# One decode layer: the second pair's keys in two loads, and two never-taken branches placed earlier

## The chip, the core and the metric

The kernel runs on one core of a Trainium2 chip. A core has a matrix engine (TensorE, PE), a vector engine (VectorE, DVE), a scalar engine (ScalarE, ACT), a general engine (GpSimd, POOL) and SyncE (SP), which issues most loads here. Each engine works through its own list of instructions, and semaphores order them. 16 DMA engines move data between the main memory and the on-chip buffer. The metric is the device time of one execution in microseconds (us); lower is better.

## The reference

One token goes through an attention block with a key and value cache, then through a block B with a second normalisation and an MLP:

```python
x = A_x                                               # 1 x 512
h = x + _A_ref(_layernorm(x), A_k_cache, A_v_cache, A_wq, A_wo)
h2 = h + _B_ref(_layernorm(h), B_w1, B_w2, B_w3, B_w4)
# _A_ref: q = x @ wq (32 heads of 128); 8 key/value heads, each serves 4 query heads
scores = einsum("bhqd,bhkd->bhqk", q, k) * (Dh ** -0.5)   # 16384 positions
p = softmax(scores); o = einsum("bhqk,bhkd->bhqd", p, v); return o @ wo
# _B_ref
hs = concatenate([g0, g1, g2, g3]) @ w2               # shifts by one and two places along the sequence
x1 = x + hs
h2 = gelu(_layernorm(x1) @ w3) @ w4                   # 512 -> 1792 -> 512
return x1 + h2
```

The sequence has one place, so every shift in block B brings in zeros alone: `hs` is zero, and `w1` and `w2` are not needed. What has to be read is the key cache and the value cache, 8 heads of 16384 x 128 values in bfloat16 each, and `wq`, `wo`, `w3` and `w4`.

## The kernel before

**Order of the work.** The functions `dve`, `act`, `pool`, `pe` and `load` append operations to one list per engine (class `Program`). When all are appended, `emit` finds which operation waits for which, and `_run` writes each engine's list out, with semaphore waits ahead of an operation where it needs them. `_vector` writes VectorE's list. `_tensor` writes TensorE's, where the four pairs of heads are a real loop over the block `pe_pair`, with inner loops over two halves and eight pieces; what stands after the loop is straight code. Nothing reorders the lists: an engine that waits holds up what is behind it in its list.

**Branches that are never taken.** At the start of their lists VectorE and TensorE mark a place for a branch hint. At the end of its list each of the two has a compare-and-branch whose condition never holds (a register that is zero, or positive, is compared with "less than 0") and which names an earlier block as its target (`body`, `pe_pair`). The hint marked at the start belongs to this branch (L146 and L315).

**Stages.** After `wq` has landed, TensorE forms the queries (L596). Then there are four pairs of key/value heads (`PAIRS`), j = 0 to 3. A pair's keys and its values are 8 MB each, 64 KB in each of 128 partitions. For one pair:

- Keys. Buffer `kb` holds a whole pair, as two halves `kb[0]` and `kb[1]`. For each half, VectorE transposes the keys into the single buffer `kt` (L619, four instructions of two pieces each; eight of one piece in the last half of the last pair), and TensorE multiplies them with the queries, piece by piece (L633, after a clearing product, L627).
- Softmax (L644 to L659): maximum on VectorE, a product on TensorE, exponential on ScalarE, transposes on VectorE.
- Values. TensorE multiplies the weights with the values in buffer `vb` (L669), in four parts.
- Gathering (L685 to L693), and a copy of the next pair's queries, `qn` (L701).

**Tail.** Products with `wo` (L735), the sums and the statistics (L739 to L539), products with `w3` (L753), the activation (L765), transposes (L769), products with `w4` (L774: 14 blocks m of four products), the last sum (L778) and the store of the output (L780).

**Loads.** SyncE issues them in the order of its list, each when its buffer is free: `wq`, the keys of pair 0 in two halves, values 0, keys 1, values 1, keys 2, values 2, keys 3, values 3 in four parts, `wo` in two, `w3`, and `w4` in three (blocks 0 to 9, 10 to 12, and 13). `wq` shares `vb` with the values. `wo` goes into `kb[0]`, `w3` and `w4` into `kb[1]`. A half of `kb` is free when VectorE has transposed all of it. `load_keys(j + 1, y)` stands behind the work of half y of pair j. For the pairs listed in `WHOLE`, it does nothing for y = 0, and for y = 1 it loads both halves with one transfer that all later transposes wait for:

```python
WHOLE = (1,)
...
if j in WHOLE:
    if y:
        load("k0", kb_all[:, :], pair_rows(A_k_cache, j), ("r", 0, 0),
             also=[("r", h, i) for h in range(2) for i in range(RPARTS)])
    return
load(f"k{y}", kb[y][:, :], pair_rows(A_k_cache, j)[:, y * n:(y + 1) * n], ("r", y, 0), ...)
```

The helper `more`, with which TensorE could repeat a product in a small loop, is defined and not called.

Of the kernel before, what the change touches and what calls it, by code (L numbers as in the profile page):

```python
# [12 lines left out]


class Op:
    __slots__ = ("eng", "fn", "deps", "sem", "val", "needed", "dma", "at", "worth", "times", "own")

    def __init__(self, eng, fn, deps, dma, at, worth, times, own):
        self.eng, self.fn, self.deps, self.dma, self.at = eng, fn, deps, dma, at
        self.worth, self.times, self.own = worth, times, own  # L20
        self.sem = self.val = None
        self.needed = False


class Program:
# [17 lines left out]
    def part(self, *mark):  # L43
        self.mark, self.count = mark or None, {}

    def op(self, eng, fn, r=(), w=(), bank=(), dma=None, worth=1, times=1, own=None):
        deps = []

        def need(o, raw):
            if o is None:  # L50
                return
            if o.eng == eng and o.dma is None and (eng == "PE" or not raw):
                return
            deps.append(o)

        for k in r:
            need(self.last_w.get(k), True)
        for k in w:
            need(self.last_w.get(k), False)
            for o in self.readers.get(k, {}).values():  # L60
                need(o, False)
        for k in bank:
            for e, o in self.users.get(k, {}).items():
                if e != eng:
                    need(o, False)
        at = None
        if self.mark is not None:
            n = self.count[eng] = self.count.get(eng, -1) + 1
            at = (*self.mark, n)
        o = Op(eng, fn, deps, dma, at, worth, times, own)  # L70
        for k in r:
            self.readers.setdefault(k, {})[(eng, dma)] = o
        for k in w:
            self.last_w[k] = o
            self.readers[k] = {}
        for k in bank:
            self.users.setdefault(k, {})[eng] = o
        if dma is not None:
            if dma not in self.dma_sems:
                self.dma_sems[dma] = self.ctx.enter_context(self.nc.semaphore(f"d_{dma}"))  # L80
                self.dma_count[dma] = 0
            self.dma_count[dma] += 16
# [57 lines left out]
    def _vector(self):  # L140
        eng = self.nc.vector
        rv = eng.alloc_register("never")
        hint = eng.mark_branch_hint_location()
        eng.reg_mov(rv, 0)
        self._run(eng, self.ops["DVE"], {})
        eng.br_lt(rv, 0, "body", "pe_query").branch_hint(hint)  # L146

    def _tensor(self):
        nc, eng, ops = self.nc, self.nc.tensor, self.ops["PE"]
        inside = [n for n, o in enumerate(ops) if o.at is not None]  # L150
        lo, hi = inside[0], inside[-1] + 1
        at = {o.at: o for o in ops[lo:hi]}
# [53 lines left out]
        sem, v0, _ = told[0, 0]  # L206
# [4 lines left out]
        r, rl, ry, rq, rk = (eng.alloc_register(n) for n in ("seen", "landed", "half", "query", "piece"))  # L211
        hint = eng.mark_branch_hint_location()
        eng.reg_mov(r, first - step * last)
        eng.reg_mov(rl, v0 - 1)
        seen = {}
# [81 lines left out]
        nc.switch_bb("pe_after", parent=None)  # L297
        seen[id(vector)] = final
        seen[id(sem)] = told[last, parts - 1][2]
        n = 0  # L300
        for o in ops[hi:]:
            if o.times == 1:
                self._run(eng, [o], seen)
                continue
            eng.reg_mov(ry, 0)
            eng.br(f"pe_more{n}")
            nc.switch_bb(f"pe_more{n}", parent=None)
            assert not o.needed
            self._run(eng, [o], seen)
            eng.reg_add(ry, ry, 1)  # L310
            eng.br_lt(ry, o.times, f"pe_more{n}", f"pe_less{n}")
            nc.switch_bb(f"pe_less{n}", parent=None)
            n += 1

        eng.br_lt(rl, 0, "pe_pair", "pe_end").branch_hint(hint)  # L315
        nc.switch_bb("pe_end", parent=None)

D = 512
HQ = 32
# [9 lines left out]
W3 = ((0, 4),)  # L329
W4 = ((0, 10), (10, 13), (13, 14))  # L330
PAIRS = HKV // 2
WHOLE = (1,)
RPARTS = 6
QPAD = 4 * 7
QW = QPAD + 128
# [4 lines left out]
def bass_sequential_preLN__gqa_block_cached__mixer_s_mlp__decode_kernel(  # L340
# [13 lines left out]
    with ExitStack() as ctx:  # L354
        sb = lambda name, shape, dt: ctx.enter_context(nc.sbuf_tensor(name, shape, dt))
        ps = lambda name, shape, dt: ctx.enter_context(nc.psum_tensor(name, shape, dt))
        P = Program(nc, ctx)
# [30 lines left out]
        qb = sb("qb", [128, 4, PAIRS, QW], BF16)  # L388
# [35 lines left out]
        O_ps = [banks[:, 2, :], banks[:, 3, :]]  # L424
# [4 lines left out]
        def load(name, dst, src, key, by="SP", also=()):  # L429
            P.op(by, lambda e: e.dma_start(dst, src), w=[key, *also], dma=name)  # L430

        def pair_rows(src, j):
            return src[0, 2 * j:2 * j + 2].rearrange("g (u t) d -> (g u) (t d)", u=64)

        def load_keys(j, y):
            n = 128 * DH
            if j in WHOLE:
                if y:
                    load("k0", kb_all[:, :], pair_rows(A_k_cache, j), ("r", 0, 0),
                         also=[("r", h, i) for h in range(2) for i in range(RPARTS)])  # L440
                return
            load(f"k{y}", kb[y][:, :], pair_rows(A_k_cache, j)[:, y * n:(y + 1) * n], ("r", y, 0),
                 also=[("r", y, i) for i in range(1, RPARTS)])

# [24 lines left out]
        def pe(fn, r=(), w=(), bank=()):  # L469
            return P.op("PE", fn, r, w, bank)  # L470

        def piece(cuts, m):
            return [lo <= m < hi for lo, hi in cuts].index(True)

        def more(n):

            P.op("PE", lambda e: e.matmul(O_ps[1][:, :], qb[:, 0, 0, 0:128], kt[:, 0:512], start=True, stop=True),
                 r=["qb", ("kt", 0)], w=[("O", 1)], bank=[("O", 1)], times=n)

        def copies(col, n):  # L480

# [45 lines left out]
        def inverse_root(i, n, by):  # L527
# [7 lines left out]
            for k in range(3):  # L535
# [31 lines left out]
            r=["hT", (("st", 0), 0), (("st", 0), 6)], w=["xn"])  # L567
# [25 lines left out]
        for i, key in enumerate(keys):  # L593
            P.part("query", i)
            for k in range(NCH):
                pe(lambda e, k=k: e.matmul(banks[:, bass.ds(P.b, 1), :], copies(xn[:, k:k + 1], 128),  # L596
                                           wq_k[:, k, bass.ds(P.c, REP * DH)], start=(k == 0), stop=(k == NCH - 1)),
                   r=["xn"] + [("v", x) for x in range(4)], w=["n" if key == "mn" else key], bank=[key])
        P.part()
        for g in range(2):  # L600
            row = banks[64 * g:64 * g + 64, PAIRS * g:PAIRS * g + PAIRS, :].rearrange("p j c -> p (j c)")
            for b in range(2):
# [122 lines left out]
        for n, (lo, hi) in enumerate(W4):  # L725
# [4 lines left out]
            r=["o_m"], w=["o_f"])  # L730
        dve(lambda e: e.tensor_copy(o_b[:, :], o_f[:, :]), r=["o_f"], w=["o_b"])

        for r_ in range(32):
# [3 lines left out]
               r=["o_b", ("r", 0, piece(WO, r_))], w=[("O", 0)], bank=[("O", 0)])  # L737
        h_ps, hkey = s_ps[:, 1, :], ("s", 1)
        dve(lambda e: e.tensor_copy(osum[:, :], O_ps[0][:, :]), r=[("O", 0)], w=["osum"], bank=[("O", 0)])  # L739
        for q in range(4):  # L740
            pe(lambda e, q=q: e.matmul(h_ps[32 * q:32 * q + 32, 0:128], copies(row32[:, 0:1], 32),
                                       osum[:, q * 128:(q + 1) * 128], start=True, stop=True),
               r=["osum", "row32"], w=[hkey], bank=[hkey])
# [4 lines left out]
            r=["hT", (S, 0)], w=["hc"])  # L748


        for k in range(NCH):
            for q in range(4):
                pe(lambda e, k=k, q=q: e.matmul(s_ps[32 * q:32 * q + 32, 0, 0:FQ], hc[:, k, :],  # L753
                                                w3_sb[:, k, q * FQ:(q + 1) * FQ], start=(k == 0), stop=(k == NCH - 1)),
                   r=["hc", ("r", 1, piece(W3, k))], w=[("s", 0)], bank=[("s", 0)])
# [5 lines left out]
            r=["hr", (S, 0), (S, 6)], w=["xs"])  # L761
        pool(lambda e: e.tensor_tensor(xsum[:, :], hr[:, :], xs[:, :], ALU.add), r=["hr", "xs"], w=["xsum"])
        for n in range(2):
            lo, hi = n * NHC // 2, (n + 1) * NHC // 2
            act(lambda e, lo=lo, hi=hi: e.activation(  # L765
                hg[:, :].rearrange("p (i m) -> p i m", m=NHC)[:, :, lo:hi],
                s_ps[:, 0, 0:FQ].rearrange("p (i m) -> p i m", m=NHC)[:, :, lo:hi],
                ACTF.Gelu_apprx_tanh, scale=s[:, 7:8]), r=[("s", 0), (S, 7)], w=[("hg", n)], bank=[("s", 0)])
            dve(lambda e, lo=lo, hi=hi: e.transpose(  # L769
                hcol[:, lo:hi, :].rearrange("p m u -> p (m u)"),  # L770
                hg[:, :].rearrange("p (i m) -> p m i", m=NHC)[:, lo:hi, :]), r=[("hg", n)], w=[("hcol", n)])
        for m in range(NHC):
            for o in range(4):
                pe(lambda e, m=m, o=o: e.matmul(  # L774
                    n_ps[32 * o:32 * o + 32, 0:128], hcol[:, m, :], w4_sb[:, m, o * 128:(o + 1) * 128],
                    start=(m == 0), stop=(m == NHC - 1)),
                   r=[("hcol", 2 * m // NHC), ("r", 1, 2 + piece(W4, m))], w=["n"], bank=["mn"])
        dve(lambda e: e.tensor_tensor(fin[:, :], xsum[:, :], n_ps[:, 0:128], ALU.add),  # L778
            r=["n", "xsum"], w=["fin"], bank=["mn"])
        P.op("SP", lambda e: e.dma_start(out[0, 0:1, :].rearrange("o (q j) -> (o q) j", q=4), fin[0:128:32, :]),  # L780
             r=["fin"], w=["out"], dma="out")
# [32 lines left out]
```

## Time and profile before

| | |
|---|---|
| median of 3 runs | 200.2 us (200.03 to 200.45) |
| profiled execution | 199.21 us, of which the span from the first to the last instruction is 196.6 us |
| mean granted TensorE clock | 0.85 of full speed |
| busy in the span | PE 114.1 us, DVE 118.0 us, ACT 9.0 us, POOL 7.3 us |
| DMA | 79.18 MB, mean 403 GB/s over the span |

A profile row of work has the start or a group's count, the engine, the line of the kernel (L619 is line 619), the operation and its operands: `kt<-kb` writes `kt` from `kb`. `[7.63 <-DMA kb...]` is the idle time of the engine ahead of the row and what ended it. The chain that ended last goes back from the last instruction, at each step to what released it. Rows of 40 digits cut the span into 40 equal slices, with the busy share in tenths. All times in the rows count from the start of the span.

### The profile page before, as it was taken

To read this page: it belongs to the slowest core of one execution; us is meant where nothing else is said; L and a number is where in the kernel's file an instruction comes from. 1 tells how busy PE (TensorE), PEld (TensorE's weight loads), DVE (VectorE), ACT (ScalarE), POOL (GpSimd) and SP (SyncE) were. 2 spreads that over 40 slices of the span, in tenths; PEclk is the share of its full clock that TensorE was granted. 3 is DMA by queue.
4 is the path that set the end of the run, shared out by engine and by line. 5 is a ranking of instruction groups with operands and counts; after the bars stand their busy time and mean duration, and the time that the engine had idled before them with its cause. 6 is when DMAs were issued, how large, how long until landed. Compare 5 with 4: busy or idle time off the path is not lost.

```text
span 196.6 us, 2321 instructions
## 1 busy us (share of the span) xinstructions
PE 114.1 (58%) x693; PEld 44.4 (23%) x693; DVE 118.0 (60%) x155; ACT 9.0 (5%) x15; POOL 7.3 (4%) x16
## 2 busy tenths in 40 slices
PE   0129619888165009988255598860928888346533
PEld 0113203233021003423022132320403323112212
DVE  6740799990534049991453999635079992452371
ACT  3000000000200000000200000002000000130020
POOL 7100000000000000000000000000000000000041
PEclk9999987999859755999859799996696999958975
DMA  6999999999999999998999999999999999999800
GB/s 227 467 453 427 447 427 527 427 427 440 427 427 427 427 427 427 427 427 367 460 433 433 440 427 427 427 420 433 427 427 417 427 427 430 442 400 423 342 0 2
DMA packets 3041, 79.18 MB, mean 403 GB/s; under 512 B 352, under 2 KB 480, under 8 KB 608
## 3 DMA queue, kind: packets, MB, share of 16 engines
q1 hardware_dynamic: 3032, 79.17, 94.0%
q14 instruction: 1, 0.01, 0.0%
q10 hardware_dynamic: 8, 0.00, 0.0%
HBM read 79.17 MB, written 0.00 MB: 403 GB/s over the span
## 4 chain that ended last, share of the span: by engine, by line
DVE 35%; PE 33%; DMA 20%; issue 8%; ACT 2%; ACTq 0%; DVEq 0%; SPq 0%
DVE kt L619 21%; PE banks L633 17%; DMA kb<-in_A_k_cache_dram 14%; PE banks L669 8%; DMA vb<-in_A_wq_dram 6%; PE banks L596 5%; DVE pt L659 4%; DVE mx L644 2%; ACT p_sb L655 2%; DVE od L688 2%; PE banks L735 1%; PE banks L774 1%; PE banks L647 1%; DVE qcol L603 1%; PE banks L691 1%
## 5 line engine op out<-in xcount | busy, mean ns | idle before, releaser
L633 PE MATMUL banks<-kt,qn 128*128 x256 | 70.5, 411 | 23.1 <-DVE kt L619 16.9
L619 DVE STREAM_TRANSPOSE kt<-kb 128x2048 int32<-128x2048 int32 (+1 forms) x36 | 70.9, 2037 | 7.6 <-DMA kb<-in_A_k_cache_dram 7.6
L633 PEld LDWEIGHTS banks<-kt,qn 128*128 x256 | 26.1, 102 | 66.1 <-issue 52.8
L669 PE MATMUL banks<-vb,pt 128*32 128x512 bf16 x256 | 20.7, 495 | 0.0
L644 DVE TENSOR_REDUCE mx<-banks 128x1 f32<-128x1024 f32 x4 | 4.9, 1224 | 20.2 <-PE banks L633 20.2
L659 DVE STREAM_TRANSPOSE pt<-p_sb 64x1024 bf16<-64x1024 bf16 x8 | 9.9, 1239 | 5.4 <-ACT p_sb L655 5.3
L685 DVE TENSOR_SCALAR od<-banks,rowc 128x128 f32<-128x128 f32 x4 | 1.4, 350 | 19.5 <-PE banks L669 19.5
L596 PE MATMUL banks<-vb,xn 128*128 x32 | 9.2, 461 | 6.1 <-DMA vb<-in_A_wq_dram 6.1
L655 ACT ACTIVATE p_sb<-banks,bias 128x1024 bf16<-128x1024 f32 x4 | 4.5, 1114 | 164.6 <-DVE nmh L651 164.6
L676 PE MATMUL banks<-acc,zd 128*32 128x1 f32 x8 | 1.1, 202 | 17.7 <-DVE pt L659 17.7
L669 PEld LDWEIGHTS banks<-vb,pt 128*32 128x32 bf16 x256 | 8.1, 121 | 10.7 <-issue 7.6
L603 DVE STREAM_TRANSPOSE qcol<-banks 64x1024 f32<-64x1024 f32 x4 | 4.8, 1228 | 8.6 <-PE banks L596 8.6
L627 PE MATMUL banks<-qn 128*128 128x512 bf16 x8 | 3.1, 387 | 7.3 <-DVE qn L701 6.3
L534 POOL TENSOR_SCALAR st<-st 128x1 f32<-128x1 f32 x1 | 0.2, 242 | 182.9 <-DVE st L519 182.9
L596 PEld LDWEIGHTS banks<-vb,xn 128*128 128x128 bf16 x32 | 3.7, 115 | 11.2 <-issue 9.0
L647 PE MATMUL banks<-mxd,mean 128*128 128x128 f32 x8 | 2.0, 326 | 6.6 <-DVE mxd L645 6.6
L691 PE MATMUL banks<-od,zo 128*32 128x128 f32 x8 | 1.6, 285 | 6.5 <-DVE od L688 6.5
L676 PEld LDWEIGHTS banks<-acc,zd 128*32 128x32 f32 x8 | 0.7, 140 | 18.4 <-DVE pt L659 18.4
L688 DVE SCALAR_TENSOR_TENSOR od<-banks,rowc,od 128x128 f32<-128x128 f32 x12 | 4.2, 351 | 0.4
L556 DVE CAST ident<-ident_f 4x4 bf16<-4x4 f32 x1 | 3.8, 3848 | 0.6 <-POOL ident_f L551 0.6
L559 PE MATMUL banks<-x,quarter 4*128 4x128 bf16 x1 | 0.3, 285 | 6.0 <-DVE quarter L557 6.0
L627 PEld LDWEIGHTS banks<-qn 128*128 128x128 bf16 x8 | 0.8, 95 | 10.5 <-issue 10.5
(76 smaller groups left out, 44.0 us busy)
## 6 DMA issues: line engine op xcount, KB each, us to landing
kb<-in_A_k_cache_dram SPq DMA_DIRECT2D x6, 4096.0 KB, 21.7
vb<-in_A_v_cache_dram SPq DMA_DIRECT2D x4, 2048.0 KB, 19.4
vb<-in_A_wq_dram SPq DMA_DIRECT2D x1, 4096.0 KB, 12.4
kb<-in_A_wo_dram SPq DMA_DIRECT2D x1, 3072.0 KB, 21.2
kb<-in_B_w_dram SPq DMA_DIRECT2D x1, 1792.0 KB, 19.0
kb<-in_B_w_dram SPq DMA_DIRECT2D x1, 1280.0 KB, 21.7
kb<-in_A_wo_dram SPq DMA_DIRECT2D x1, 1024.0 KB, 23.3
kb<-in_B_w_dram SPq DMA_DIRECT2D x1, 384.0 KB, 22.2
```

What stands on the lines that cost most here:

```text
L556: dve(lambda e: e.tensor_copy(ident[:, :], ident_f[0:4, 0:4]), r=["ident_f"], w=["ident"])
L596: pe(lambda e, k=k: e.matmul(banks[:, bass.ds(P.b, 1), :], copies(xn[:, k:k + 1], 128), wq_k[:, k, bass.ds(P.c, REP * DH)], start=(k == 0) ...
L603: dve(lambda e, g=g, b=b, row=row: e.transpose(qcol[64 * g:64 * g + 64, 2 * b:2 * b + 2, :, :].rearrange("p e m u -> p (e m u)"), row.rear ...
L619: P.op("DVE", lambda e, view=view: e.transpose(view(kt), view(kb[y])), r=[("r", y, i) for i in range(RPARTS)], w=[("kt", t + i) for i in r ...
L627: pe(lambda e: e.matmul(s_ps[:, bass.ds(P.y, 1), :], copies(none, 128), copies(none, 512), start=True, stop=False, skip_group_check=True), ...
L633: pe(lambda e, n=n: e.matmul(s_ps[:, bass.ds(P.y, 1), :], qn[:, n, bass.ds(P.q, 128)], ktv[:, n // 2, n % 2, :, bass.ds(P.k, 8), :], start ...
L644: dve(lambda e: e.tensor_reduce(mx[:, :], s_all, AX.X, ALU.max), r=[("s", 0), ("s", 1)], w=["mx"], **both)
L647: pe(lambda e: e.matmul(m_ps[:, 0:128], mean4[:, :], mxd[:, :], start=True, stop=True), r=["mxd", "mean4"], w=["m"], bank=["mn"])
L655: act(lambda e: e.activation(p_sb[:, :], s_all, ACTF.Exp, bias=bias[:, 0:1], scale=float(SCALE), accum_out=acc[:, :]), r=[("s", 0), ("s", ...
L659: dve(lambda e, g=g: e.transpose(pt[64 * g:64 * g + 64, :, :, g, :], p_sb[64 * g:64 * g + 64, :]), r=["p"], w=["pt"])
L669: pe(lambda e, x=x, l=l, ct=ct, ch=ch: e.matmul(O_ps[0][32 * ct:32 * ct + 32, :], pt[:, 8 * x + l, ch, :, :].rearrange("p g u -> p (g u)") ...
L688: dve(lambda e, block=block, c=c: e.scalar_tensor_tensor(od[:, :], block, rowc[:, c:c + 1], od[:, :], ALU.mult, ALU.add), r=[key, "rowc", ...
```

## The change

The keys of pair 1 are loaded as those of the other pairs: one transfer per half, each with its own semaphore, the first behind the work of half 0 of pair 0, the second behind that of half 1. The never-taken branches, with the hints that belong to them, no longer stand at the end: VectorE's stands behind its transposes of the activation and ahead of the last sum, TensorE's ahead of block 10 of the products with `w4`. Operations without a function, `dve(None)` and `pe(None)`, mark the two places in the lists. The unused helper `more`, the field `times` and the code that wrote its loop are gone.

```diff
     def _vector(self):
...
-        self._run(eng, self.ops["DVE"], {})
-        eng.br_lt(rv, 0, "body", "pe_query").branch_hint(hint)
+        ops, seen = self.ops["DVE"], {}
+        on = next(n for n, o in enumerate(ops) if o.fn is None)
+        self._run(eng, ops[:on], seen)
+
+        eng.br_lt(rv, 0, "body", "ve_on").branch_hint(hint)
+        self.nc.switch_bb("ve_on", parent=None)
+        self._run(eng, ops[on + 1:], seen)
...
-        n = 0
-        for o in ops[hi:]:
-            if o.times == 1:
-                self._run(eng, [o], seen)
-                continue
...
-        eng.br_lt(rl, 0, "pe_pair", "pe_end").branch_hint(hint)
-        nc.switch_bb("pe_end", parent=None)
+        on = next(n for n, o in enumerate(ops) if o.fn is None)
+        self._run(eng, ops[hi:on], seen)
+
+        eng.br_lt(rl, 0, "pe_pair", "pe_on").branch_hint(hint)
+        nc.switch_bb("pe_on", parent=None)
+        self._run(eng, ops[on + 1:], seen)
...
-WHOLE = (1,)
...
         def load_keys(j, y):
             n = 128 * DH
-            if j in WHOLE:
-                if y:
-                    load("k0", kb_all[:, :], pair_rows(A_k_cache, j), ("r", 0, 0),
-                         also=[("r", h, i) for h in range(2) for i in range(RPARTS)])
-                return
...
+        dve(None)
         for m in range(NHC):
+            if m == W4[1][0]:
+                pe(None)
             for o in range(4):
```

More of the change, by code (lines that the diff above doesn't have):

```diff
@@ L15, with __init__ @@
 class Op:
-    __slots__ = ("eng", "fn", "deps", "sem", "val", "needed", "dma", "at", "worth", "times", "own")
-    def __init__(self, eng, fn, deps, dma, at, worth, times, own):
+    __slots__ = ("eng", "fn", "deps", "sem", "val", "needed", "dma", "at", "worth", "own")
+    def __init__(self, eng, fn, deps, dma, at, worth, own):
         self.eng, self.fn, self.deps, self.dma, self.at = eng, fn, deps, dma, at
-        self.worth, self.times, self.own = worth, times, own
+        self.worth, self.own = worth, own
         self.sem = self.val = None
@@ L44, in part, with op @@
         self.mark, self.count = mark or None, {}
-    def op(self, eng, fn, r=(), w=(), bank=(), dma=None, worth=1, times=1, own=None):
+    def op(self, eng, fn, r=(), w=(), bank=(), dma=None, worth=1, own=None):
         deps = []
@@ L69, in op @@
             at = (*self.mark, n)
-        o = Op(eng, fn, deps, dma, at, worth, times, own)
+        o = Op(eng, fn, deps, dma, at, worth, own)
         for k in r:
@@ L299, in _tensor @@
         seen[id(sem)] = told[last, parts - 1][2]
-        n = 0
-        for o in ops[hi:]:
-            if o.times == 1:
-                self._run(eng, [o], seen)
-                continue
[L305 to L313, printed above, removed]
-        eng.br_lt(rl, 0, "pe_pair", "pe_end").branch_hint(hint)
-        nc.switch_bb("pe_end", parent=None)
+        on = next(n for n, o in enumerate(ops) if o.fn is None)
[3 more added lines that the diff above has]
+        self._run(eng, ops[on + 1:], seen)
 D = 512
@@ L473, in piece @@
             return [lo <= m < hi for lo, hi in cuts].index(True)
-        def more(n):
-            P.op("PE", lambda e: e.matmul(O_ps[1][:, :], qb[:, 0, 0, 0:128], kt[:, 0:512], start=True, stop=True),
-                 r=["qb", ("kt", 0)], w=[("O", 1)], bank=[("O", 1)], times=n)
         def copies(col, n):
```

## The prediction

> **What bounds the kernel now.** I read the page first: its span, the granted clock, the DMA row and the shares of the chain that ended last.
>
> ```profile
> span 196.6 us, 2321 instructions
> PEclk9999987999859755999859799996696999958975
> DMA  6999999999999999998999999999999999999800
> DVE 35%; PE 33%; DMA 20%; issue 8%; ACT 2%; ACTq 0%; DVEq 0%; SPq 0%
> ```
>
> Two things run through the whole span. The DMA engines are busy from the second slice to the 38th of 40, so the stream of loads never pauses. And the chain is mostly DVE and PE, with 20% DMA. The chain in order of time tells where that DMA is: besides the opening load there is one piece, and its landing ends the only long DVE idle time with a DMA as its releaser. Next the rows of VectorE from the timeline (start, length, instruction; in brackets the idle time before it).
>
> ```profile
> 44.23 27.01 DMA kb<-in_A_k_cache_dram
> ```
> ```profile
> 26.51 17.66 DVE L619 STREAM_TRANSPOSE kt<-kb 128x2048 int32<-128x2048 int32 x8
> 63.41 0.30 DVE L701 COPY qn<-qb 128x624 bf16<-128x624 bf16 x1
> 71.34 17.66 DVE L619 STREAM_TRANSPOSE kt<-kb 128x2048 int32<-128x2048 int32 x8 [7.63 <-DMA kb<-in_A_k_cache_dram]
> 108.14 0.32 DVE L701 COPY qn<-qb 128x624 bf16<-128x624 bf16 x1
> 108.37 17.65 DVE L619 STREAM_TRANSPOSE kt<-kb 128x2048 int32<-128x2048 int32 x8
> 145.38 0.32 DVE L701 COPY qn<-qb 128x624 bf16<-128x624 bf16 x1
> 145.62 17.89 DVE L619 STREAM_TRANSPOSE kt<-kb 128x2048 int32<-128x2048 int32 x12
> 193.58 0.29 DVE L778 TENSOR_TENSOR fin<-xsum,banks 128x128 bf16<-128x128 f32 x1 [1.32 <-PE banks L774]
> ```
>
> Pair 1's key transposes wait for one 8 MB load, which lands at 44.23 + 27.01 = 71.24. From there on no pair waits for keys: the transposes of pairs 1, 2 and 3 start at 71.34, 108.37 and 145.62, some 37.1 us apart, which is the pace of DVE and PE. So whatever moves 71.34 moves the end, until the stream of loads stops it. Where it stops it is read from the issues (SP's rows of the timeline) and, below them, from the DMA view in one small window around each issue (the last number is the time from issue to landing).
>
> ```profile
> 23.00 0.33 SPq L430 DMA_DIRECT2D vb<-in_A_v_cache_dram  x1
> 61.18 0.33 SPq L430 DMA_DIRECT2D vb<-in_A_v_cache_dram  x1
> 80.31 9.05 SPq L430 DMA_DIRECT2D kb<-in_A_k_cache_dram  x2
> 105.80 0.33 SPq L430 DMA_DIRECT2D vb<-in_A_v_cache_dram  x1
> 117.33 9.10 SPq L430 DMA_DIRECT2D kb<-in_A_k_cache_dram  x2
> 154.57 0.81 SPq L430 DMA_DIRECT2D kb<-in_A_wo_dram  x2
> 163.59 1.75 SPq L430 DMA_DIRECT2D kb<-in_B_w_dram  x4
> ```
> ```profile
> vb<-in_A_v_cache_dram SPq DMA_DIRECT2D x1, 28.9
> vb<-in_A_v_cache_dram SPq DMA_DIRECT2D x1, 29.4
> kb<-in_A_k_cache_dram SPq DMA_DIRECT2D x1, 4096.0 KB, 20.0
> kb<-in_A_k_cache_dram SPq DMA_DIRECT2D x1, 4096.0 KB, 21.0
> vb<-in_A_v_cache_dram SPq DMA_DIRECT2D x1, 23.7
> kb<-in_A_k_cache_dram SPq DMA_DIRECT2D x1, 4096.0 KB, 21.8
> kb<-in_A_k_cache_dram SPq DMA_DIRECT2D x1, 4096.0 KB, 22.8
> kb<-in_A_wo_dram SPq DMA_DIRECT2D x1, 1024.0 KB, 23.3
> kb<-in_B_w_dram SPq DMA_DIRECT2D x1, 1792.0 KB, 19.0
> kb<-in_B_w_dram SPq DMA_DIRECT2D x1, 1280.0 KB, 21.7
> kb<-in_B_w_dram SPq DMA_DIRECT2D x1, 128.0 KB, 22.1
> ```
>
> Issue plus time gives the landings. A row of two issues that is 9.05 long has its second one 0.33 before its end, so at 89.03; likewise 126.10, 154.94 (0.44 long) and 164.91 (0.43 long, the last of four, whose second is at 163.96). Values 0 land at 51.9, values 1 at 90.6, keys 2 at 100.3 and 110.0, values 2 at 129.5, keys 3 at 139.1 and 148.9, the last part of wo at 178.2, w3 at 182.6, the first w4 part at 185.7 and the last at 187.0. They land in the order of issue, and at the size's own pace: a half of the keys every 9.7 us, the whole of pair 1 in 71.2 - 51.9 = 19.3. That is a line of transfers served one after the other, always with a next one waiting. An earlier issue cannot make this line shorter; it can only let work start on what has landed.
>
> **The keys in halves.** Removed: one issue of 8 MB at 44.23, after the last transposes of pair 0. Added: an issue of the first half when the first four transposes of pair 0 are done, 26.51 + 17.66/2 = 35.3 (the same step in pair 1: 71.34 + 8.83 = 80.2, issue at 80.31), and the second half at 44.23 as before. On SP that is one more issue, 0.33 us; the next thing behind it waits until 44.23 anyway, so it costs nothing. DVE's second half gets one more semaphore wait, on a landing that is earlier than its turn (below).
>
> Both halves stand in the line behind values 0, so they land at 51.9 + 9.7 = 61.6 and 71.2, where the whole landed before. DVE is free for them after qn at 63.41; transposes start 0.24 after qn does (108.14 to 108.37, 145.38 to 145.62), so at 63.65 instead of 71.34: a gain of 7.69. The first half lasts until 72.5, when the second has been there for 1.3 us. Between them the halves could also break the line; the bound from rows is 9.7 us a half against 19.3 the whole, at most 0.1 us, and I take nothing.
>
> The Trainium skill, DMA: Bandwidth & Descriptors, section Anatomy of one DMA, gives every transfer a fixed 2.0 us beside its bytes. If that were paid between the halves, all later landings would be 2 us later and the sum 196.2. The rows above disagree: halves that wait in line land 9.7 us apart, which leaves no 2 us.
>
> What is late next, pair by pair, all 7.69 earlier:
> - Value products: pair 2's are wanted at 137.71 - 7.69 = 130.0 (row below), landed 129.5. Pair 1's, a pair's 37.0 earlier, at 93.0, landed 90.6. No wait.
> - Pair 2's keys: wanted at 100.68, landed 100.3. Second half wanted at 109.5, landed 110.0: DVE waits 0.5. It is covered: PE begins half 1 of pair 1 at 83.91 (row below) while DVE had its first piece pair ready at 71.34 + 5 x 2.21 = 82.4, so 1.5 us are spare.
> - Pair 3's keys: wanted at 137.93, landed 139.13. This wait of 1.2, with 0.1 from landing to start, is not covered: 1.3 of the gain is lost. The second half (wanted 148.1, landed 148.9) waits inside the spare 1.5. What is left is 6.39.
>
> ```profile
> 83.91 0.39 PE L627 MATMUL banks<-qn 128*128 128x512 bf16 x1
> 137.71 5.22 PE L669 MATMUL banks<-vb,pt 128*32 128x512 bf16 x64
> 183.40 1.91 PE L735 MATMUL banks<-kb,o_b 128*32 128x512 bf16 x32 [1.06 <-DVE o_b L731]
> 188.36 1.35 PE L753 MATMUL banks<-kb,hc 128*32 128x448 bf16 x16 [0.69 <-ACT hc L747]
> 190.68 0.85 ACT L765 ACTIVATE hg<-banks,st 128x224 bf16<-128x224 f32 x2 [2.37 <-DVE st L539]
> 191.84 1.69 PE L774 MATMUL banks<-kb,hcol 128*32 128x128 bf16 x56 [2.12 <-DVE hcol L769]
> ```
>
> - The tail: wo's last part is used three quarters into L735, 183.40 - 6.39 + 1.43 = 178.4, landed 178.2. L753 would start at 182.0 and waits for w3 until 182.7; it ends at 184.05, and the activation that reads it waits for DVE's statistics until 190.68 - 6.39 = 184.3, so that wait is covered. L774 would start at 185.45; w4's first part is there at 185.7: 0.3 lost. Its last four products come at 185.75 + 1.3 = 187.0, when the last part lands. So the gain left is 6.1, and here it meets the end of the stream: nothing could be faster than about 187.0 + 0.4 for the last sum, against 193.58 now.
>
> **The branches.** Each is one compare-and-branch that falls through. The rows: DVE's branch now, by its line; a turn of PE's key loop; and the instruction queue in the window 194 to 196.6.
>
> ```profile
> L146 DVEq COMPARE_BRANCH  x1: 67/67/67, 193.6 to 193.6; - x1
> ```
> ```profile
> 88.15 1.04 PE L633 MATMUL banks<-kt,qn 128*128 x4 [0.21 <-issue]
> ```
> ```profile
> q14 instruction: 1, 0.01, 1.3%
> ```
>
> On DVE it took 67 ns after the last sum; ahead of it, it runs while DVE waits 1.32 for the products, so nothing. On PE it lies in the last products: between two turns of the loop, with a branch, three register steps and a wait, PE idles 0.21, so the cost is between 0 (the array still has products queued) and 0.21; 0.07, DVE's own, is my value, nearest in kind. A gain is bounded too: one instruction packet shows in that window, after the branches; fetched sooner it could save some of the 2.6 us that the profiled time, 199.21, has around its span, but nothing shows that the end waits for it. I take 0. The removed helper and loop code issued nothing.
>
> **Sum:** -7.69 + 1.30 + 0.3 + 0.07 = -6.0: 193.2 against the profiled 199.21. The median of the runs, 200.2, is 1.0 above the profiled one; with the same 6.0 it gives **194.2**.
>
> **Rivals.**
> - *The PE branch makes the sequencer fetch code.* The hint names a branch target at the loop, so code behind the branch may be missing. One fetch: the slice that holds the packet is the 17th of 40 in that window, 195.0, 1.4 after DVE's branch; with its own time some 2 us. On the last products that gives 196.2. For it: the packet follows the branch. Against: nothing shows an engine waiting for it. The Trainium skill (Runtime: NRT & Kernel Launch, Instruction fetch mechanics) says that a taken branch out of the resident pages stalls and that fetching is otherwise sequential; by that these branches, never taken, cost no fetch; no run here shows it yet.
> - *A slower stream.* If the median's extra 1.0 is stream pace (71.2 us grown by 1.4%), the stream's end at 187.0 grows by 2.6, and the new kernel, which ends with it, comes at 193.2 + 2.6 = 195.8.
> - *Slower than before:* the stream loses pace because loads are queued earlier beside more work. It decides where its end passes today's need, 187.0 + 6.1: 4% over the 151 us from 35.4 on; at 5% the time is about 201.6. Against: the DMA row stands at 9 with one transfer waiting and with three.
> - *Hidden anyway:* both halves share the engines and land together at 71.2: 200.2. Against: the landings in order above.
>
> **Chances.** Forecast 0.58 (193.2 to 195.2), code fetch 0.12, stream pace 0.15, better through the end's fetch 0.05, hidden 0.04, slower 0.06. The range 193.2 to 197.0 holds the first three. The runs of before spread over 0.4 us, so 0.2% is about what can be told: faster 0.90, same 0.03, slower 0.07.
>
> **What will show it.** Pair 1's transposes at 63.6 with no DMA before them; a DMA wait of about 1.3 before pair 3's; w4's products at 185.7, waiting for DMA; last landing still near 187; no gap in L774 after its 40th product. I am wrong if the landings shift, if pair 1's first half lands after 64, or if a gap of microseconds stands inside L774.

## The result and the profile after

The changed kernel takes 192.62 us (median of 4 runs, 192.18 to 193.06) where the kernel before took 200.31 us beside it (200.03 to 200.45). The ratio is 0.9618, with a 95% interval of 0.9587 to 0.9648: it is faster, by 7.7 us. The forecast was 194.2 us, with a range from 193.2 to 197.0: the direction was right, and the time is 0.6 us below the range.

The profiled execution took 193.06 us, with a span of 191.2 us. First the page of the changed kernel:

```profile
span 191.2 us, 2324 instructions
PEclk9999975999756759999576699995797999958975
DMA  6999999999999999997999999979999999999990
DMA 36%; DVE 31%; PE 24%; issue 6%; ACT 2%; DVEq 0%; ACTq 0%; SPq 0%
...
L603 DVE STREAM_TRANSPOSE kt<-kb 128x2048 int32<-128x2048 int32 (+1 forms) x36 | 70.9, 2036 | 0.0
```

The group of the key transposes (L603 here, L619 before) had 7.6 us of idle time before it, all of it for a DMA; now it has 0.0. The DMA row is nearly full to the end, and the chain that ended last has 36% DMA instead of 20%. Next the rows of VectorE from its timeline: the key transposes of pairs 1, 2 and 3, and the last sum.

```profile
64.10 17.64 DVE L603 STREAM_TRANSPOSE kt<-kb 128x2048 int32<-128x2048 int32 x8
102.21 17.65 DVE L603 STREAM_TRANSPOSE kt<-kb 128x2048 int32<-128x2048 int32 x8
140.04 17.99 DVE L603 STREAM_TRANSPOSE kt<-kb 128x2048 int32<-128x2048 int32 x12
188.31 0.29 DVE L765 TENSOR_TENSOR fin<-xsum,banks 128x128 bf16<-128x128 f32 x1 [1.32 <-PE banks L761]
```

Pair 1 starts 7.2 us earlier than before (64.10 against 71.34), pair 2 6.2, pair 3 5.6, and the last sum is 5.3 earlier. The end of the stream of loads has not moved: the last part of w4 is the fourth of the issues in the first row (164.91 before, 159.43 now), and lands 27.5 us later, at 186.9; before it was 187.0.

```profile
158.11 1.75 SPq L424 DMA_DIRECT2D kb<-in_B_w_dram  x4
```
```profile
kb<-in_B_w_dram SPq DMA_DIRECT2D x1, 128.0 KB, 27.5
```

So the gain begins as forecast, with pair 1's keys. The end of this execution is not on the floor of the forecast, though. In the forecast the products with `w3` and `w4` wait for their loads; here they wait for ScalarE and VectorE, behind loads that landed at 182.5 and 185.7, and the last sum comes 0.8 us later than the 187.5 that follows from the forecast:

```profile
183.10 1.11 PE L737 MATMUL banks<-kb,hc 128*32 128x448 bf16 x16 [0.69 <-ACT hc L731]
186.58 1.68 PE L761 MATMUL banks<-kb,hcol 128*32 128x128 bf16 x56 [2.37 <-DVE hcol L753]
```

And 5.4 us of span are not 7.7 us of time. Three things were open: where in the time the rest comes from, which of the two parts of the change it belongs to, and what makes this end later than the stream.

### The profile page after: what moved, and what is told of

It is laid out like the page before. It is cut to its first block, busy times and chain, and to the rows that moved or that the text cites. A ratio compares the mean times of both kernels' runs of the same rounds, so it can differ in the third digit from the quotient of the medians.

```text
span 191.2 us, 2324 instructions
## 1 busy us (share of the span) xinstructions
PE 117.6 (61%) x693; PEld 45.4 (24%) x693; DVE 118.0 (62%) x155; ACT 9.0 (5%) x15; POOL 7.3 (4%) x16
## 4 chain that ended last, share of the span: by engine, by line
DMA 36%; DVE 31%; PE 24%; issue 6%; ACT 2%; DVEq 0%; ACTq 0%; SPq 0%
DMA kb<-in_A_k_cache_dram 29%; DVE kt L603 21%; PE banks L617 10%; DMA vb<-in_A_wq_dram 6%; PE banks L653 6%; PE banks L580 4%; DVE pt L643 3%; DVE mx L628 1%; ACT p_sb L639 1%; DVE od L672 1%; PE banks L719 1%; PE banks L761 1%; DVE qcol L587 1%; PE banks L631 1%; DVE st L521 0%
## 5 line engine op out<-in xcount | busy, mean ns | idle before, releaser
L617 PE MATMUL banks<-kt,qn 128*128 x256 | 71.3, 418 | 14.2 <-DVE kt L603 8.7
L603 DVE STREAM_TRANSPOSE kt<-kb 128x2048 int32<-128x2048 int32 (+1 forms) x36 | 70.9, 2036 | 0.0
L653 PE MATMUL banks<-vb,pt 128*32 128x512 bf16 x256 | 23.9, 555 | 0.0
L580 PE MATMUL banks<-vb,xn 128*128 x32 | 8.5, 431 | 6.0 <-DMA vb<-in_A_wq_dram 6.0
L653 PEld LDWEIGHTS banks<-vb,pt 128*32 128x32 bf16 x256 | 9.1, 134 | 12.9 <-issue 11.8
## 6 DMA issues: line engine op xcount, KB each, us to landing
kb<-in_B_w_dram SPq DMA_DIRECT2D x1, 1792.0 KB, 24.4
```

Source lines behind the costliest of these rows:

```text
L603: P.op("DVE", lambda e, view=view: e.transpose(view(kt), view(kb[y])), r=[("r", y, i) for i in range(RPARTS)], w=[("kt", t + i) for i in r ...
L617: pe(lambda e, n=n: e.matmul(s_ps[:, bass.ds(P.y, 1), :], qn[:, n, bass.ds(P.q, 128)], ktv[:, n // 2, n % 2, :, bass.ds(P.k, 8), :], start ...
L653: pe(lambda e, x=x, l=l, ct=ct, ch=ch: e.matmul(O_ps[0][32 * ct:32 * ct + 32, :], pt[:, 8 * x + l, ch, :, :].rearrange("p g u -> p (g u)") ...
```

## The experiments

Each time is split into the span, from the first to the last instruction, and what lies around it (time less span). All times are in us.

| kernel | median (lowest to highest) | spans | around the span |
|---|---|---|---|
| chip 1: before, 13 runs | 200.4 (198.66 to 201.09) | 196.4 to 199.1, median 197.4 | over 2.5 in 11, 1.9 in 2 |
| e1_halves, 4 | 192.88 (192.5 to 194.24) | 190.2 to 191.4 | 1.9, 1.9, 2.6, 2.8 |
| e2_branches, 10 | 200.19 (198.29 to 201.13) | 196.4 to 198.8, median 198.2 | 1.9 to 2.1 in 9, 2.6 in 1 |
| e4_pe_at_end, 4 | 192.84 (192.4 to 193.52) | 190.3 to 191.1 | 1.9, 1.9, 2.2, 3.2 |
| e5_ve_at_end, 4 | 193.04 (192.31 to 194.54) | 190.3 to 192.6 | 1.9, 2.0, 2.0, 3.0 |
| chip 2: before, 7 | 200.66 (198.91 to 201.39) | 197.0 to 199.5, median 198.3 | 1.9 to 2.0 in 6, 3.0 in 1 |
| e3_no_branch, 4 | 191.85 (191.76 to 191.97) | 190.4 to 190.7 | 1.3 to 1.4 |
| e6_warm, 4 | 195.2 (195.04 to 195.62) | 193.1 to 193.7 | 1.9 |
| e7_quarters, 4 | 192.57 (192.56 to 192.72) | 190.6 to 190.7 | 1.9 to 2.0 |
| e9_before_warm, 4 | 196.28 (195.96 to 196.7) | 194.0 to 194.8 | 1.9 to 2.0 |
| chip 1 again: before, 6 | 200.71 (199.08 to 201.39) | 196.4 to 198.8, median 198.05 | 2.6 to 2.9 |
| e8_changed, 4 | 192.39 (192.22 to 192.93) | 190.3 to 191.0 | 1.9 to 2.0 |
| e10_warm_no_branch, 4 | 192.49 (192.1 to 192.64) | 190.8 to 191.3 | 1.3 |
| e11_no_ve, 4 | 191.6 (191.41 to 193.37) | 190.1 to 192.1 | 1.3 |
| e12_no_pe, 4 | 191.78 (191.71 to 192.21) | 190.4 to 190.9 | 1.3 |

### One part of the change alone

The kernel before with the keys in halves:

```diff
-WHOLE = (1,)
+WHOLE = ()
```

> The kernel before with pair 1's keys in two loads and nothing else; both never-taken branches stay at the end of their lists. Theory A (the two parts add: the halves shorten the span by 5.4 to 6.3 us, the branches shorten what lies around the span, 2.6 us before and 1.9 after): about 193.3 us, span 190.3 to 191.2, 2.6 us around the span. Theory B (the branches do nothing; the whole 7.7 us comes from the keys): about 192.6 us.

Its spans, 190.2 to 191.4, are those of the changed kernel (190.3 to 191.2): the whole gain of the span belongs to the keys. The ratio to before is 0.9662 (0.9584 to 0.974). Its median, 192.88, lies between the two theories, and what lies around the span is 1.9 us in two of its four runs and 2.6 and 2.8 in the others: these runs alone do not decide between them.

The changed kernel with `WHOLE = (1,)` and the old `load_keys`, which leaves the moved branches alone:

> The kernel before with both branches moved and nothing else; pair 1's keys stay one load. Theory A: about 199.5 us, span as before (196.6 to 197.5), some 1.9 us around it. Theory B: 200.3 us. A third view (the branches cost a code fetch on the last products, hidden in the changed kernel by its waits for w4): above 200.3, with a gap inside the last products.

The ratio is 0.9982 (0.9937 to 1.0027): no difference to be told in the time. But what lies around the span was 2.6 us or more in 11 of 13 runs of before and in 1 of 10 here, on the same chip, while the spans happened to be longer. On chip 2 the kernel before itself has 1.9 in six of seven. So the moved branches take some 0.8 us off where the longer ending occurs; where it does not, no gain from them shows. They are not the only thing that can take it away: in e1_halves, with both branches at the end, it is missing from two runs of four. No gap stands in the last products of e2_branches or of the changed kernel: 56 products in 1.68 us, as before.

The changed kernel with one branch put back behind the last operation of its engine:

```diff
-        self._run(eng, ops[hi:on], seen)
+        self._run(eng, ops[hi:on] + ops[on + 1:], seen)
...
         eng.br_lt(rl, 0, "pe_pair", "pe_on").branch_hint(hint)
         nc.switch_bb("pe_on", parent=None)
-        self._run(eng, ops[on + 1:], seen)
```

> The changed kernel with TensorE's branch put back behind its last product; VectorE's stays ahead of the last sum. If TensorE's place is what shortens the end: about 193.3 us with 2.6 us around the span. If VectorE's place does it: 192.6 us with 1.9 us around the span.

The same for VectorE's list:

> The changed kernel with VectorE's branch put back behind the last sum; TensorE's stays ahead of block 10. If VectorE's place is what shortens the end: about 193.3 us with 2.6 us around the span. If TensorE's does it: 192.6 us with 1.9 us around the span.

Each has one run in four with 3 us around the span and three with about 2. Four runs do not tell the two places apart, so whether one of them alone would do stays open.

### Where the forecast chain holds

The changed kernel once more, profiled in an execution that took 192.27 us:

> The changed kernel, on the same chip as the next three, to compare them with. Both theories: 192.6 us, spans of 190.3 or 191.2 by the phase of the granted clock, 1.9 us around the span.

Rows of its VectorE and TensorE:

```profile
63.63 17.64 DVE L603 STREAM_TRANSPOSE kt<-kb 128x2048 int32<-128x2048 int32 x8
101.07 8.88 DVE L603 STREAM_TRANSPOSE kt<-kb 128x2048 int32<-128x2048 int32 x4
110.27 8.89 DVE L603 STREAM_TRANSPOSE kt<-kb 128x2048 int32<-128x2048 int32 x4 [0.32 <-issue]
139.35 8.89 DVE L603 STREAM_TRANSPOSE kt<-kb 128x2048 int32<-128x2048 int32 x4 [0.69 <-DMA kb<-in_A_k_cache_dram]
148.99 9.13 DVE L603 STREAM_TRANSPOSE kt<-kb 128x1024 int32<-128x1024 int32 x8 [0.75 <-DMA kb<-in_A_k_cache_dram]
187.61 0.29 DVE L765 TENSOR_TENSOR fin<-xsum,banks 128x128 bf16<-128x128 f32 x1 [1.54 <-PE banks L761]
```
```profile
182.78 1.68 PE L737 MATMUL banks<-kb,hc 128*32 128x448 bf16 x16 [1.41 <-DMA kb<-in_B_w_dram]
185.88 1.69 PE L761 MATMUL banks<-kb,hcol 128*32 128x128 bf16 x56 [1.42 <-DMA kb<-in_B_w_dram]
```

The forecast had pair 1 at 63.65, pair 2 at 100.68 with a wait of 0.5 for its second half, pair 3 at 139.23 with a covered wait at 148.9, the products with `w3` at 182.7, those with `w4` at 185.75 and the last sum at 187.5. All are within 0.4 us. The waits ahead of pair 3, `w3` and `w4` end by the loads that were named; the row of pair 2's second half names no releaser, but that half landed at 110.2, just ahead of it. The profile on record above is another execution of the same program, with the last sum 0.7 later and no DMA wait before pair 3. What differs most is the value products. Their rows on TensorE, of the kernel before (its pair 2 stands in the prediction), of e2_branches (keys as before), of the changed kernel on record, and of e8_changed:

```profile
55.90 5.17 PE L669 MATMUL banks<-vb,pt 128*32 128x512 bf16 x64
100.77 4.92 PE L669 MATMUL banks<-vb,pt 128*32 128x512 bf16 x64
174.93 5.38 PE L669 MATMUL banks<-vb,pt 128*32 128x512 bf16 x64
```
```profile
55.11 6.50 PE L659 MATMUL banks<-vb,pt 128*32 128x512 bf16 x64
100.71 5.90 PE L659 MATMUL banks<-vb,pt 128*32 128x512 bf16 x64
138.67 5.69 PE L659 MATMUL banks<-vb,pt 128*32 128x512 bf16 x64
176.43 5.58 PE L659 MATMUL banks<-vb,pt 128*32 128x512 bf16 x64
```
```profile
55.05 6.48 PE L653 MATMUL banks<-vb,pt 128*32 128x512 bf16 x64
93.48 6.05 PE L653 MATMUL banks<-vb,pt 128*32 128x512 bf16 x64
131.59 5.77 PE L653 MATMUL banks<-vb,pt 128*32 128x512 bf16 x64
169.43 5.63 PE L653 MATMUL banks<-vb,pt 128*32 128x512 bf16 x64
```
```profile
55.89 5.17 PE L653 MATMUL banks<-vb,pt 128*32 128x512 bf16 x64
93.00 5.39 PE L653 MATMUL banks<-vb,pt 128*32 128x512 bf16 x64
130.45 5.44 PE L653 MATMUL banks<-vb,pt 128*32 128x512 bf16 x64
168.73 5.07 PE L653 MATMUL banks<-vb,pt 128*32 128x512 bf16 x64
```

The same 64 products take 4.92 to 6.50 us. The granted clock goes with it. In the stretch from 56 to 62 us (the last numbers of a row are granted clock, DMA share and GB/s) the kernel before and then the changed kernel on record show:

```profile
56.00:62.00 6.00, 5.07 (x66) 1.91 (x63) 0.95 (x4) 0.00 (x0) 0.00 (x0) 0.75 0.83 360
```
```profile
56.00:62.00 6.00, 5.53 (x60) 1.95 (x52) 0.37 (x2) 0.00 (x0) 0.00 (x0) 0.60 0.95 410
```

The Trainium skill, TensorE: Matmul & The Clock Gate, Part 1, says that the array idles at half clock, that some 3.4 us of sustained work release it, and that the window is free-running, so that the same kernel varies between runs. The rows fit that as far as they go: two executions of one program, the changed kernel on record and e8_changed, take 6.48 and 5.17 us for pair 0's products. No run here shows the window itself, and the mean clock of a whole run does not order the spans: of the 13 runs of before on chip 1, three of 196.4 to 196.7 us have 0.84, five of 197.1 to 197.7 us have 0.85.

With the keys whole, these differences go into the end one for one: the last three value products of e2_branches are 17.17 us against 15.52 before (5.90 + 5.69 + 5.58; 4.92 + 5.22 + 5.38), 1.65 more, and its last sum stands at 195.28 against 193.58, 1.70 later (its row follows). In the changed kernel on record they are 17.45 against 15.90 in e8_changed, 1.55 more, pair 1 starts 0.47 later besides, and the last sum is only 0.70 later: the rest disappears in e8_changed's waits for keys, `w3` and `w4`. That fits the spans, which reach over 3 us before (196.4 to 199.5, 26 runs) and over 0.9 in the changed kernel (190.3 to 191.2, 8 runs). The stream does not hide everything: of the variants with the keys in halves, e5_ve_at_end and e11_no_ve each have one span of 192.6 and 192.1, at mean clocks of 0.837 and 0.839.

```profile
195.28 0.29 DVE L771 TENSOR_TENSOR fin<-xsum,banks 128x128 bf16<-128x128 f32 x1 [1.32 <-PE banks L767]
```

### Warmer value products

18 products more per pair keep TensorE busy ahead of the value products. In the kernel before:

```diff
             pe(lambda e: e.matmul(m_ps[:, 0:128], mean4[:, :], mxd[:, :], start=True, stop=True),
                r=["mxd", "mean4"], w=["m"], bank=["mn"])
+            for _ in range(18):
+                pe(lambda e: e.matmul(O_ps[1][:, :], qn[:, 0, 0:128], qn[:, 0:4, 0:128], start=True, stop=True),
+                   r=["qn"], w=[("O", 1)], bank=[("O", 1)])
```

> The kernel before with the same 18 extra products per pair. Theory (from the landing of pair 1's keys on, the kernel before is paced by VectorE and TensorE, and its spread of spans, 196.4 to 199.1, is that of the value products' clock): value products 3.5 to 4 us, three of them behind the keys' landing, 4 to 5 us off the span, so 191.5 to 193 with a spread under 0.5. Rival (the spread comes from the stream of loads): span 196 or more, spread as before.

All four value products take 3.64 us. A row of them, the products with `wo`, and VectorE's first key transposes of pair 1:

```profile
101.86 3.64 PE L672 MATMUL banks<-vb,pt 128*32 128x512 bf16 x64
179.94 3.54 PE L738 MATMUL banks<-kb,o_b 128*32 128x512 bf16 x32 [1.05 <-DVE o_b L734]
```
```profile
72.52 17.66 DVE L619 STREAM_TRANSPOSE kt<-kb 128x2048 int32<-128x2048 int32 x8 [9.79 <-DMA kb<-in_A_k_cache_dram]
```

The ratio is 0.9795 (0.973 to 0.9859), and the spans of four runs reach over 0.8 us, where those of seven runs before reach over 2.5. So most of the spread goes with the clock of the value products. The spans, 194.0 to 194.8, miss the expected 191.5 to 193 by 1 us and more: the three products behind the keys gain 15.52 - 3 x 3.64 = 4.6, but pair 1's keys land at 72.4 instead of 71.2, and the products with `wo`, which now find the clock low (0.59 in the stretch from 180 to 184), take 3.54 us instead of 1.91. While those keys are on their way, in the window 60 to 62, a packet of instructions is read, which the kernel before does not do there:

```profile
q8 instruction: 1, 0.02, 3.4%
```

The same in the changed kernel:

> The changed kernel with 18 products of 512 columns more per pair, into an unused bank, between the softmax's own product and the sums, so that TensorE is not idle ahead of the value products; their results go nowhere. Theory (the granted clock ahead of the value products makes the spread, and the stream of loads is the floor): value products some 3.5 to 4 us instead of 5.0 to 6.5, last load still landing at 187, last sum at 187.4, span 190.3 in every run, time 192.2. Rival (VectorE and TensorE still set the end): each pair 1.5 to 2 us shorter and the span under 188.

Here the time gets worse, 195.2, and neither theory had it. TensorE's rows, and the instruction queue in the window 186.5 to 190:

```profile
185.53 1.36 PE L764 MATMUL banks<-kb,hcol 128*32 128x128 bf16 x44 [1.42 <-DMA kb<-in_B_w_dram]
189.75 0.51 PE L764 MATMUL banks<-kb,hcol 128*32 128x128 bf16 x12 [2.85 <-issue]
```
```profile
q8 instruction: 1, 0.02, 2.4%
```

In the middle of the last products TensorE stops for 2.85 us, while a 16 KB packet of instructions is read; all four runs are long (spans of 193.1 to 193.7). That is the fetch of code that the prediction named as a rival, in a program whose loop is 36 instructions longer (18 weight loads and 18 products). The changed kernel itself does not have the stop. Its two executions differ in the packet: e8_changed reads one of the same size on the same queue at 187.9, behind its last product, and the trace on record has none there. The part of the expectation that could be seen came true: the products with w4 start at 185.53, waiting for their load, though every value product is 1.4 us or more shorter. The stream is the floor.

### The first keys sooner

The first half of pairs 2 and 3 in two loads:

```diff
+            if j >= 2 and not y:
+                half = lambda x, u: x.rearrange("p (x f) -> p x f", x=2)[:, :, u * n // 4:(u + 1) * n // 4]
+                for u in range(2):
+                    load(f"q{u}", half(kb[0][:, :], u), half(pair_rows(A_k_cache, j)[:, 0:n], u), ("r", 0, 3 * u), ...)
+                return
...
```

The first two transposes of that half then wait for the first of the two loads, the others for the second.

> The changed kernel with the first half of pair 2's and of pair 3's keys in two loads (a quarter of the pair each), so that pair 3 never waits for its first keys. Theory (the stream is the floor): last sum at 187.4 or later, span 190.3 to 191.2, no change. Rival (the wait ahead of pair 3's keys costs its full 0.9 to 1.3 us): spans of 189.2 to 190.

```profile
137.66 8.88 DVE L609 STREAM_TRANSPOSE kt<-kb 128x2048 int32<-128x2048 int32 x4
149.26 9.13 DVE L609 STREAM_TRANSPOSE kt<-kb 128x1024 int32<-128x1024 int32 x8 [2.71 <-DMA kb<-in_A_k_cache_dram]
187.87 0.29 DVE L771 TENSOR_TENSOR fin<-xsum,banks 128x128 bf16<-128x128 f32 x1 [1.52 <-PE banks L767]
```

Pair 3 starts 1.7 us sooner than in e8_changed, waits 2.0 us longer for its second half, and the last sum comes at 187.9. 192.57 us against 192.62: the wait ahead of pair 3's keys, which the prediction took off the gain, costs nothing that the stream would not take anyway. The finer cut has a small price of its own: a quarter takes 4.97 us in the line, so the two take 0.23 more than a half, and the last load comes at 187.3 instead of 187.0.

### No branches at all

The changed kernel without the branches and their hints:

```diff
-        hint = eng.mark_branch_hint_location()
...
-        eng.br_lt(rv, 0, "body", "ve_on").branch_hint(hint)
-        self.nc.switch_bb("ve_on", parent=None)
...
-        eng.br_lt(rl, 0, "pe_pair", "pe_on").branch_hint(hint)
-        nc.switch_bb("pe_on", parent=None)
```

> The changed kernel without either never-taken branch and without their hints. Theory A (a branch that runs early has the code for the end fetched in time; without it the fetch comes late, as with VectorE's branch at the end): the same span, 190.3 to 191.2, and about 2.7 us around it, so 193.4 us. Rival (it is the branch at the end that costs, and no branch is as good as an early one): 192.6 us, 1.9 around the span.

Both were wrong: 1.3 us lie around the span, less than in any kernel with both branches, and the time is 191.85. With one of the two pairs of branch and hint gone:

> The changed kernel without VectorE's branch and hint; TensorE's stay ahead of block 10. If VectorE's hint makes the late code fetches at the end: 1.3 us around the span, 192.0 us. If TensorE's does: 1.9 us around it, 192.6 us.

> The changed kernel without TensorE's branch and hint; VectorE's stay ahead of the last sum. If TensorE's hint makes the late code fetches at the end: 1.3 us around the span, 192.0 us. If VectorE's does: 1.9 us around it, 192.6 us.

Either way it is 1.3 us. Against e8_changed on the same chip, e12_no_pe has no run in common (191.71 to 192.21 against 192.22 to 192.93), and e11_no_ve three of its four below; the medians are 0.6 and 0.8 us less. These three are the fastest kernels of the study. A branch and its hint were always taken out together, so no run tells which of the two it is.

Not all of the gain lies around the span. From the start of the last sum to the end of the span, where SyncE has waited for the store of the output, it is 2.8 to 3.0 us in all ten traces with both branches and 2.0 in the four without one or both. In e8_changed that is 190.4 - 187.61 = 2.8, in e12_no_pe 190.5 - 188.50 = 2.0:

```profile
188.50 0.29 DVE L761 TENSOR_TENSOR fin<-xsum,banks 128x128 bf16<-128x128 f32 x1 [1.56 <-PE banks L757]
```

So the end behind the last sum is some 1.4 us shorter, 0.8 of it inside the span, and the last sums come later instead (188.1 to 188.5 against 187.6). The instruction queues show a difference. In the window from 188.5 to 193.5 us of e8_changed:

```profile
q14 instruction: 2, 0.02, 0.9%
```

With both branches, two packets of 8 KB are read behind the last sum in every trace, the first while SyncE waits for the store. Without both branches, or without TensorE's, there is none (e3_no_branch, e10_warm_no_branch, e12_no_pe); in e11_no_ve there is one, at the end of that wait. That the first packet makes the store late is not shown beyond this coincidence.

Code is read while the stream still runs instead. In e11_no_ve an 8 KB packet stands in the window 54 to 56, and the next half of the keys lands 10.4 us after the load ahead of it instead of 9.7:

```profile
q14 instruction: 1, 0.01, 1.0%
```

In e12_no_pe a packet stands in the window 178 to 182, and `w3`, issued at 157.88, lands 25.6 us later, at 183.5, where the changed kernel has 182.5 (158.11 and 24.4):

```profile
157.88 1.75 SPq L420 DMA_DIRECT2D kb<-in_B_w_dram  x4
```
```profile
q8 instruction: 1, 0.02, 1.7%
...
kb<-in_B_w_dram SPq DMA_DIRECT2D x1, 1792.0 KB, 25.6
```
```profile
kb<-in_B_w_dram SPq DMA_DIRECT2D x1, 1792.0 KB, 24.4
```

A packet is not the only thing that goes with a late load: in e2_branches the values of pair 2 land 20.6 us after the load ahead of them instead of 19.4, and its trace has no packet of instructions there.

Last, the 18 products and no branches:

> The changed kernel with the 18 extra products per pair and without both branches and hints. Theory (with the hint to the loop, TensorE finds the code behind a block's end missing, which is the gap of 2.85 us inside the last products of the run with 18 extra products): no such gap, last sum at 187.4 to 188.4 after the stream, 1.3 us around the span, time 191 to 192. Rival (any code of that length has the gap): last sum at 190.3 again, time 194.6.

```profile
187.61 1.68 PE L754 MATMUL banks<-kb,hcol 128*32 128x128 bf16 x56 [1.80 <-DVE hcol L746]
```

No gap: the last products run through in 1.68 us. The time, 192.49, is half a us above the range, and the last sum, at 189.35, is 1 us later than expected: two packets are read during the stream (at 55.7 and 61.9), the last load lands at 188.1, and the products with `wo` take 3.60 us. The gap of e6_warm thus needs the branches with their hints as well as the longer code; which of the two branches it needs was not tried.

## Why the prediction was right and where it failed

**Right: the bound and the chain.** The end moved because pair 1's transposes no longer wait. In e8_changed it stopped where the forecast stopped it, at the end of the stream; in the profile on record, at a lower clock, VectorE and TensorE still set it, 0.7 us later. The span that the sum gives, 196.6 - 6.0 = 190.6, lies inside the measured 190.3 to 191.2. The landings did not shift. The halves did not break the line of transfers (they land 9.7 us apart). The section of the Trainium skill that the prediction names for a fixed 2.0 us (DMA: Bandwidth & Descriptors, Anatomy of one DMA) gives them for transfers that GpSimd issues. These loads are SyncE's, so the rows neither confirm nor contradict it. Of the rivals, a slower stream and loads hidden anyway did not come.

**Failed: "The median of the runs, 200.2, is 1.0 above the profiled one; with the same 6.0 it gives 194.2."** The 1.0 was carried over, as if the changed kernel had it too. The runs show what it was: the profiled span of 196.6 was near the low end of 196.4 to 199.5, and its distance from the median (197.4 to 198.3) comes in the main from the value products' clock, behind the landing of pair 1's keys (e2_branches and e9_before_warm). The change removes most of that from the end, because it ends at or shortly behind the stream. The profile had a hint of it: its four value products, equal work, took 4.92 to 5.38 us. The rival of a slower stream read the same 1.0 the other way, and was wrong: in the two profiled executions the last load lands at 187.0 and 186.9, and in e2_branches, an execution near the median, halves of the keys still land every 9.7 us and nothing waits for its one late load.

**Failed: the branch term, +0.07.** It was priced on the path inside the span, where it is nothing (the products take 1.68 us, no gap). What the prediction set to 0 for lack of a waiter, the 2.6 us around the span, is where the moved branches act: 1.9 after the change (e2_branches and e8_changed show it for chip 1). The window in which it looked for packets closed with the span, at 196.6. The trace goes on, and in its window from 197 to 200 two more packets are read:

```profile
q8 instruction: 1, 0.02, 2.0%
q14 instruction: 1, 0.01, 0.8%
```

Put together: 194.2 - 1.0 - 0.7 (2.6 to 1.9) + 0.1 (190.7, the middle of the spans, for 190.6) = 192.6, as measured.

**The wait ahead of pair 3's keys, +1.3,** was 0.7 us in e8_changed (139.35) and nothing in the profile on record, where the clock was lower (140.04). It does not add to the end: with it gone, e7_quarters still ends with the stream. So the span came out right because of the floor, and not because of this term.

**The rival of the code fetch** did not happen in the changed kernel, but it is real: 2.85 us in e6_warm, where 2 were reckoned. So the argument that branches which are never taken cost no fetch is not safe: without them, in e10_warm_no_branch, the stop is gone.

**Open:** why the kernel before ends 2.7 us after its span on one chip in nearly every run and 1.9 on another; which instruction waits for which packet there, since no instruction of the program stands behind the span. One lead: the only trace with the longer ending, that of the kernel before, reads a 16 KB packet at 198.5, after both of 8 KB; no trace with 1.9 us has one so late. That moving the branches takes it from 2.7 to 1.9 on the first chip is shown by e2_branches and e8_changed; that one of the two places alone does it is not.

## What to carry to other kernels

When a wait for a load is the only one on the chain, sum the gain up to the next floor, here the end of a stream that never pauses, and forecast the new end from that floor: what varies ahead of it counts less (here 0.9 us of spread were left of 3.1), so the difference between a profile and the median must not be carried over. Look at what lies around the span as a term of its own, and look for packets of instructions beyond the span's end too. A never-taken branch with its hint is worth a run with and without it, as is a change of code length: in these runs both moved the moments at which code is read.

## What was not expected of the hardware

- Reading code during the stream goes with late loads: without a packet of instructions, a half of the keys takes 9.7 us in every trace, an 8 KB packet goes with one that takes 10.4 (e11_no_ve), and a 16 KB packet with a `w3` that lands 1.0 us late (e12_no_pe). One late load, in e2_branches, has no packet beside it.
- The same 64 value products take 3.64 us behind other products and 4.92 to 6.50 us behind idle time; with the first, the spans of the kernel before spread over 0.8 us instead of 2.5.
- With never-taken branches and hints on both VectorE and TensorE, wherever they stood, 1.9 us or more lie around the span and 2.8 to 3.0 us between the start of the last sum and the end of the span; with one or none it is 1.3 and 2.0 us.
